# One PSUM tensor of eight banks instead of two fixed groups, with a new task order, in a rope-attention and mixer kernel

## The chip, the core and the metric

The kernel runs on one core of a Trainium2 chip. The metric is device time in microseconds of one execution. Time before: 646.65 us, the median of 3 runs (645.56 to 647.14).

The engines are PE (matrix products), DVE (vector), ACT (scalar and exponential), POOL (general) and SP (issues transfers). They run side by side and wait for each other on semaphores. PE writes its results into PSUM, which has eight banks of 512 floats in each of 128 partitions; DVE and ACT empty a bank, and PE can use it again only then.

## What is computed

```
q, k, v: (4 batches, 8 heads, 576 positions, 64)
q_rot, k_rot = rotate(q), rotate(k)            # x1*cos - x2*sin, x1*sin + x2*cos
scores = (q_rot @ k_rot^T) / sqrt(64)
attn = exp(scores - max);  attn = attn / (sum(attn) + 1e-9)
x = (attn @ v), heads side by side: (4, 576, 512)
h = relu(x^T @ w_tok1) @ w_tok2;  u = x + h^T   # token mixer, width 256
out = u + relu(u @ w_ch1) @ w_ch2               # channel mixer, width 1536
```

The mixer weights come as 64-bit floats and are split on the chip into a high and a low part of 32 bits (`f64_split`); products that need the accuracy take three passes, high by high, high by low and low by high.

## The kernel before, in words

**Two programs, one after the other.** `attention` and the splitting of the token weights (`tok_weights`) are planned together; then `mixers` runs the token and the channel mixer. Each is a list of tasks. `Plan.run` replays the list with estimated durations: on each engine it takes, among the tasks that can start within `SLACK` of the first possible start, the one with the lowest priority number, and emits it. The order of instructions on every engine is fixed by that. The priorities are 9 times the number of the pair plus a number out of the table `AT`.

**Pairs.** The 32 heads are worked on two at a time: 16 pairs, numbered from 0. In this document the tasks of a pair have short names (lines of the kernel before):

- uk and uq: k and q, rotated by POOL (by DVE for pair 0, in two parts: rows 0 to 1 and rows 2 to 4 of a partition; lines 303 to 309), are turned by ten PE transposes (L332); ACT writes the high part (L346), DVE the low part (L349). Until DVE has read it, the bank is held.
- S0, S1, S2, S3: scores of 128 positions of both heads, 12 matmuls each (L431). Each fills two scores tiles, and a scores tile is two banks. DVE's "mx" (L384) copies a scores tile to SBUF, negates it and finds the maximum; that frees the two banks. ACT's "ex" (L388) then makes the exponentials.
- SN: scores of the last 64 positions of both heads, 6 matmuls into one scores tile (L402).
- T0a, T0b to T3a, T3b and TN: transposes of the exponentials, 8, 10 and 10 of them (L451, L413), each task into two single banks. One copy for each bank takes them to SBUF (L456, L418, L422), on ACT or on DVE as the planner thinks it ends first.
- PV0, PV1: attention times v (L469), into one bank; one copy takes it out (L472). In the trace one such matmul is two rows.
- F: the result is turned back by ten transposes (L498) and scaled by DVE (L503, L507).

**Banks.** The scores have two tiles of two banks of their own (`s_ps`), taken in turn; everything else shares four single banks (`t_ps`). So two scores tiles at most are in flight, and four of the others.

**Start.** Tables of cosine and sine come in two transfers from ACT's queue, one pair for k and one (with the factor 1/8 of the scores in it) for q, and four small transfers for the last rows (lines 245 to 248). The q, k and v of a pair come from SP's queue, a large transfer and two small ones each (L278, L282, L285).

## Time and profile before

| | us |
|---|---|
| median of 3 runs | 646.65 |
| the profiled execution, its own time | 648.51 |
| its span, first to last instruction | 646.7 |
| PE busy in the span | 610.4 (94%) |
| DVE busy | 436.4 (67%) |
| ACT busy | 320.6 (50%) |
| POOL busy | 210.5 (33%) |

How to read it: attention fills the first 272 us and the mixers the rest. Busy shares over the whole span mix the two. A PE that counts as busy may be doing matmuls at half rate or issuing them with small gaps between, so the places where PE stands are read from the starts of its instructions in order of time.

### The profile page before, as it was taken

The numbers are of one execution on the slowest core, as the hardware profiler recorded it, in microseconds if no ns is written. First come the engines' busy times: TensorE is split into PE (matmuls) and PEld (weight loads), VectorE is DVE, ScalarE is ACT, GpSimd is POOL, SyncE is SP. The second block draws the span as 40 slices with busy tenths as digits, with TensorE's granted clock in tenths as the row PEclk, the third lists the DMA queues.
The fourth block names the chain that finished last, engine by engine and source line by source line (L and its number), as shares of the span: only waits on it lengthen the run. The fifth ranks groups of instructions, "written<-read, shape, count | busy, mean of one in ns | idle before, by whom it ended". The sixth has DMA issues, their size and how long they took to land.

```text
span 646.7 us, 13245 instructions
## 1 busy us (share of the span) xinstructions
PE 610.4 (94%) x5112; PEld 510.0 (79%) x5112; DVE 436.4 (67%) x1003; ACT 320.6 (50%) x825; POOL 210.5 (33%) x257
## 2 busy tenths in 40 slices
PE   2989999999999999799999999999999999999997
PEld 1766777777777777577879889889989988998995
DVE  4699999988788887499658896379533853233322
ACT  2789889898888888544226542124201410110110
POOL 3968888887766660123021111010000100000000
PEclk9999999999999999989999999999999999999999
DMA  6632322222222020021001422013000100001212
GB/s 181 184 93 61 95 69 60 62 61 80 62 61 61 21 94 3 1 64 59 1 11 64 122 74 58 0 66 96 35 1 1 65 1 0 1 1 65 82 50 98
DMA packets 33439, 36.57 MB, mean 57 GB/s; under 512 B 13792, under 2 KB 26848, under 8 KB 33376
## 3 DMA queue, kind: packets, MB, share of 16 engines
q1 hardware_dynamic: 32512, 35.01, 18.5%
q8 instruction: 40, 0.66, 0.4%
q10 hardware_dynamic: 864, 0.72, 0.3%
q14 instruction: 23, 0.19, 0.1%
HBM read 31.00 MB, written 4.72 MB: 55 GB/s over the span
## 4 chain that ended last, share of the span: by engine, by line
PE 52%; DVE 4%; ACT 1%; issue 0%; POOL 0%; ACTq 0%
PE m L740 22%; PE m L763 22%; PE m L679 3%; PE m L657 3%; DVE xs L640 1%; PE m L718 1%; DVE fh L545 0%; DVE fh L551 0%; DVE rs L665 0%; DVE fa L549 0%; DVE X L682 0%; DVE c1l L558 0%; DVE ul L721 0%; DVE fa L543 0%; DVE fa L547 0%
## 5 line engine op out<-in xcount | busy, mean ns | idle before, releaser
L742 ACT ACTIVATE gh<-m 128x384 fp32r<-128x384 f32 x72 | 35.4, 492 | 188.1 <-PE m L740 158.9
L388 ACT ACTIVATE p<-p,nm 128x576 f32<-128x576 f32 x128 | 100.1, 785 | 9.6 <-DVE p L384 8.9
L384 DVE TENSOR_SCALAR_CACHE_REDUCE p<-s 128x576 f32<-128x576 f32 x128 | 94.5, 751 | 11.6 <-PE s L431 10.9
L740 PE MATMUL m<-uh,c1h 128*128 128x384 f32 x288 | 97.0, 337 | 0.0
L740 PE MATMUL m<-uh,c1l 128*128 128x384 f32 x288 | 96.6, 336 | 0.0
L740 PE MATMUL m<-ul,c1h 128*128 128x384 f32 x288 | 96.6, 335 | 0.0
L744 DVE SCALAR_TENSOR_TENSOR gl<-m,gh 128x384 fp32r<-128x384 f32 x72 | 39.9, 556 | 75.8 <-ACT gh L742 75.3
L469 PE MATMUL t<-pt,vraw 128*64 128x256 f32 (+1 forms) x640 | 85.3, 413 | 0.8 <-ACT pt L422 0.3
L763 PE MATMUL m<-c2h,gh 128*128 128x512 f32 x216 | 84.9, 393 | 0.2 <-DVE ul L721 0.2
L763 PE MATMUL m<-c2h,gl 128*128 128x512 f32 x216 | 85.1, 394 | 0.0
L763 PE MATMUL m<-c2l,gh 128*128 128x512 f32 x216 | 85.0, 393 | 0.0
L765 DVE TENSOR_TENSOR X<-m,X 128x512 f32<-128x512 f32 x64 | 44.1, 691 | 52.1 <-PE m L763 51.4
L469 PEld LDWEIGHTS t<-pt,vraw 128*64 128x64 f32 x640 | 44.4, 138 | 28.6 <-issue 0.7
L456 ACT COPY pt<-t 128x256 f32<-128x256 f32 (+1 forms) x155 | 55.8, 406 | 20.0 <-PE t L451 19.8
L451 PEld LDWEIGHTS t<-ident,p 64*128 64x128 f32 x1152 | 49.7, 141 | 18.9 <-DVE kl L349 4.7
L451 PE MATMUL t<-ident,p 64*128 64x64 f32 x1152 | 59.6, 230 | 2.3 <-ACT pt L456 1.1
L431 PE MATMUL s<-kh,qh 64*128 64x288 f32 x256 | 57.1, 348 | 1.8 <-DVE p L384 1.6
L456 DVE COPY pt<-t 128x256 f32<-128x256 f32 (+1 forms) x101 | 44.3, 451 | 16.2 <-PE t L451 15.4
L740 PEld LDWEIGHTS m<-uh,c1h 128*128 128x128 f32 x288 | 54.1, 188 | 1.1 <-ACT uh L720 0.2
L740 PEld LDWEIGHTS m<-ul,c1h 128*128 128x128 f32 x288 | 54.1, 188 | 0.9
L740 PEld LDWEIGHTS m<-uh,c1l 128*128 128x128 f32 x288 | 54.1, 188 | 0.0
L431 PE MATMUL s<-kl,qh 64*128 64x288 f32 x256 | 49.7, 309 | 0.0
(125 smaller groups left out, 1191.1 us busy)
## 6 DMA issues: line engine op xcount, KB each, us to landing
stg<-in_moe_w_ch_dram SPq DMA_DIRECT2D x16, 384.0 KB, 3.2
stg<-in_moe_w_ch_dram SPq DMA_DIRECT2D x12, 512.0 KB, 4.0
kraw<-in_k_dram SPq DMA_DIRECT2D x16, 256.0 KB, 2.8
qraw<-in_q_dram SPq DMA_DIRECT2D x16, 256.0 KB, 2.8
vraw<-in_v_dram SPq DMA_DIRECT2D x16, 256.0 KB, 3.0
out_dram<-X SPq DMA_DIRECT2D x16, 256.0 KB, 2.3
stg<-in_moe_w_tok_dram SPq DMA_DIRECT2D x4, 512.0 KB, 4.8
kraw<-in_k_dram SPq DMA_DIRECT2D x32, 32.0 KB, 2.5
```

The costliest lines, as they stand in the source:

```text
L384: return lambda: nc.vector.tensor_scalar(out=p().rearrange("p (a b) -> p a b", a=2), in0=sb.t[:, :, 0:W2], scalar1=-1.0, scalar2=None, op0 ...
L388: return lambda: nc.scalar.activation(out=p(), in_=p(), func=ACTF.Exp, bias=nm.t, scale=-1.0, accum_out=l())
L431: nc.tensor.matmul(sbs[h].t[:, c, 0:W2], flat(a.t)[halves[h], TL + j * P:TL + (j + 1) * P], flat(m.t)[halves[h], TL * (1 - h) + c * W2:TL ...
L451: nc.tensor.transpose(xy[z].t[:, i * TL:(i + 1) * TL], pb.t[halves[z], c0:c0 + P], ident[halves[z], halves[z]])
L456: return lambda: e(out=pt[c].t[:, R * h:R * h + m, o + z * TL:o + (z + 1) * TL], in_=xy[z].t[:, 0:m * TL].rearrange("p (r s) -> p r s", r=m))
L469: nc.tensor.matmul(ab.t[halves[h], 0:w], vb.t[:, h, r, :], m, start=(r == 0), stop=(r == R))
L657: nc.tensor.matmul(tb.t, a, m, start=(r == 0 and i == 0), stop=(r == R and i == len(lst) - 1))
L740: nc.tensor.matmul(tb.t[:, 0:N], a, m, start=(i == 0), stop=(i == len(lst) - 1))
L742: x = add("ACT", 0.49, lambda f=f, tb=tb: nc.scalar.activation(out=gb.t[0][:, f], in_=tb.t[:, 0:N], func=ACTF.Relu), [x], [tb, gb], pr + f)
L744: y = add("DVE", 0.56, lambda f=f, tb=tb: nc.vector.scalar_tensor_tensor(out=gb.t[1][:, f], in0=tb.t[:, 0:N], scalar=0.0, in1=gb.t[0][:, f ...
L763: nc.tensor.matmul(tb.t, a, m, start=(i == 0), stop=(i == len(lst) - 1))
L765: y = add("DVE", 0.69, lambda u=u, tb=tb: nc.vector.tensor_tensor(out=u, in0=tb.t, in1=u, op=ALU.add), [z] + sums.get((ci, x), []), [tb], ...
```

## The change

- PSUM is one tensor of eight banks (class `Banks`). A scores tile takes two neighbours beginning at an even bank, every other task takes single banks, and the planner picks the bank that is free first; for single ones at a tie it prefers a bank whose neighbour is taken.
- A scores task reserves its DVE targets (the maxima and the tile for the exponentials) when it is planned, and not when mx is.
- The two copies out of TN's bank are one task, both on the same engine.
- The tables for q are dropped: the factor 1/8 moves into mx's multiplier. What is left comes in two transfers by rows (0 to 1, then 2 to 4) and one small one that waits for both.
- The large transfer of pair 0's k is split into rows 0 to 1 and 2 to 3; its first rotation waits for the first part alone. S0 and S1 of pair 0 wait for the first part of q alone.
- `AT` and `SLACK` have new numbers (PE's slack 0.332 in place of 0.065), which gives another order on every engine. The number of PE instructions stays the same, and in the mixers PE's order has no difference.

```diff
+class Banks:
+    def __init__(self, tile, n):
+        self.tile = tile
+        self.free = {i: 0.0 for i in range(n)}
+        self.made = 0
+    def pick(self, free, two, now):
+        if two:
+            c = min(((max(x, free[i + 1]), i) for i, x in free.items() if i % 2 == 0 and i + 1 in free), default=None)
+            return c and (c[0], (c[1], c[1] + 1))
+        c = min(((max(x, now), i ^ 1 in free, x, i) for i, x in free.items()), default=None)
+        return c and (c[2], (c[3],))
...
-AT = {'load': [-830.1, -824.37, -769.97], 'rot': [-930.58, 206.32], 'pt': [-93.3, -920.53], 'bd': [-226.39], ...
+AT = {'load': [428.08, 436.6, 926.66], 'rot': [418.96, 847.53], 'pt': [599.57, 525.47], 'bd': [314.07], ...
-SLACK = {'PE': 0.065, 'ACT': 0.047, 'DVE': 0.002, 'POOL': 0.135, 'SP': 0.211}
+SLACK = {'PE': 0.332, 'ACT': 0.026, 'DVE': 0.047, 'POOL': 0.235, 'SP': 0.078}
...
-        tabs = pers.tile([P, 4, R + 1, D], F32, name="tabs")
+        tabs = pers.tile([P, 2, R + 1, D], F32, name="tabs")
...
-        s_ps = slots("s", 2, [P, 2, 512], pool=psum)
-        t_ps = slots("t", 4, [P, 512], pool=psum, fifo=False)
-        a_ps = t_ps
-        nc.scalar.dma_start(out=tabs[:, 0:2], in_=tab[0:2].rearrange("a p r d -> p a r d"))
-        nc.scalar.dma_start(out=tabs[:, 2:4], in_=tab[2:4].rearrange("a p r d -> p a r d"))
-        for j in range(4):
-            nc.scalar.dma_start(out=tabs[TL:P, j, R], in_=tab[j, 0:TL, R])
+        banks = Banks(psum.tile([P, 8, 512], F32, name="s"), 8)
+        for r0, r1 in ((0, 2), (2, R + 1)):
+            nc.scalar.dma_start(out=tabs[:, :, r0:r1], in_=tab[0:2, :, r0:r1].rearrange("a p r d -> p a r d"))
+        nc.scalar.dma_start(out=tabs[TL:P, :, R], in_=tab[0:2, 0:TL, R].rearrange("a p d -> p a d"))
...
-                l = [add("SP", 0.5, ld, bufs=[rb], prio=pl)]
+                rows = ((0, 2), (2, R)) if n == 0 and nm == "k" else ((0, R),)
+                l = [add("SP", 0.5, ld(*x), bufs=[rb], prio=pl) for x in rows]
...
-                x = l
+                x = l[0:1] if n == 0 else l
...
-                return lambda: nc.vector.tensor_scalar(out=p().rearrange("p (a b) -> p a b", a=2), in0=sb.t[:, :, 0:W2], scalar1=-1.0,
+                return lambda: nc.vector.tensor_scalar(out=p().rearrange("p (a b) -> p a b", a=2), in0=sb.t[:, :, 0:W2], scalar1=-D ** -0.5,
...
-                t = add("PE", 0.9, qk, qd + kd, [*sbs, qh, ql, kh, kl], g + AT["qk"][i], mode="row")
+                t = add("PE", 0.9, qk, qp[0 if j < 2 else -1] + kd, [*sbs, qh, ql, kh, kl, *nmb, pb], g + AT["qk"][i], mode="row")
```

**PE at the start.** Before, PE turns the second part of pair 0's q (the last rows L332) and then begins S0 (L431); `t` and `s` are the PSUM tiles.

```order
L332 MATMUL t_144<-ident,uq_100 128x64
L332 MATMUL t_145<-ident,uq_100 128x64
L431 MATMUL s_140<-kh_102,qh_106 128x288
L431 MATMUL s_141<-kh_102,qh_106 128x288
L431 MATMUL s_140<-kl_104,qh_106 128x288
L431 MATMUL s_141<-kl_104,qh_106 128x288
L431 MATMUL s_140<-kh_102,ql_108 128x288
L431 MATMUL s_141<-kh_102,ql_108 128x288
```

Now `s` is the one PSUM tensor; L367 are the transposes of k and q, L469 the scores.

```order
L367 MATMUL s<-ident,uk_99 128x64 x10
L367 MATMUL s<-ident,uq_100 128x64 x4
L469 MATMUL s<-kh_102,qh_106 128x288 x2
L469 MATMUL s<-kl_104,qh_106 128x288 x2
L469 MATMUL s<-kh_102,ql_108 128x288 x2
L469 MATMUL s<-kh_102,qh_106 128x288 x2
L469 MATMUL s<-kl_104,qh_106 128x288 x2
L469 MATMUL s<-kh_102,ql_108 128x288 x2
L367 MATMUL s<-ident,uq_100 128x64 x6
```

S0 of pair 0 has moved ahead of the six transposes of q's second part.

**DVE in a middle pair.** Before, the mx (L384) of a pair alternate with copies out of transpose banks (L456) and low parts (L349), at most two of them in a row.

```order
L487 RECIPROCAL ri_129<-l_126 128x10
L456 COPY pt_120<-t_143 128x4x64
L384 TENSOR_SCALAR p_114,nm_135<-s_140 128x576
L456 COPY pt_120<-t_143 128x4x64
L384 TENSOR_SCALAR p_114,nm_138<-s_141 128x576
L384 TENSOR_SCALAR pq_117,nm_137<-s_140 128x576
L456 COPY pt_120<-t_143 128x5x64
L456 COPY pt_120<-t_142 128x5x64
L349 TENSOR_TENSOR ql_109<-t_144,qh_107 128x5x64
L349 TENSOR_TENSOR ql_109<-t_145,qh_107 128x5x64
```

Now L421 is mx and L494 the copy.

```order
L525 RECIPROCAL ri_129<-l_126 128x10
L494 COPY pt_120<-s 128x5x64
L421 TENSOR_SCALAR p_113,nm_136<-s 128x576
L421 TENSOR_SCALAR p_113,nm_132<-s 128x576
L421 TENSOR_SCALAR p_114,nm_137<-s 128x576
L421 TENSOR_SCALAR pq_117,nm_138<-s 128x576
L421 TENSOR_SCALAR p_114,nm_139<-s 128x576
L421 TENSOR_SCALAR p_115,nm_133<-s 128x576
L421 TENSOR_SCALAR p_115,nm_135<-s 128x576
L494 COPY pt_121<-s 128x4x64
```

Seven mx of S0, S1, SN and S2 stand in a row. On PE, S0, S1, SN, S2 and PV1 of the pair before follow each other, and ACT has the seven ex in a row.

**PE between S3 and PV0 of a middle pair.** Before, between S3 of one pair (the first row) and S0 of the next (the last) stand T0b (`p_113`), T1a (`p_114`), F (`oT`) and T1b; rows of a kind that follow are left out.

```order
L431 MATMUL s_141<-kh_103,ql_109 128x288
L451 MATMUL t_142<-ident,p_113 128x64
...
L451 MATMUL t_144<-ident,p_114 128x64
...
L498 MATMUL t_142<-ident,oT_123 128x64
...
L451 MATMUL t_145<-ident,p_114 128x64
L431 MATMUL s_140<-kh_102,qh_106 128x288
```

Now the row L469 ends S3, and L507 is PV0 of the same pair.

```order
L469 MATMUL s<-kh_102,ql_108 128x288 x2
L489 MATMUL s<-ident,p_113 128x64 x10
L489 MATMUL s<-ident,p_114 128x64 x18
L450 MATMUL s<-ident,pq_117 128x64 x10
L489 MATMUL s<-ident,p_115 128x64 x18
L367 MATMUL s<-ident,uq_100 128x64 x10
L536 MATMUL s<-ident,oT_122 128x64 x10
L367 MATMUL s<-ident,uk_99 128x64 x10
L507 MATMUL s<-pt_121,vraw_97 64x256 x10
```

The transposes of the next pairs' k and q, TN, F and all of T0b to T2b stand in one run of 86; before, the longest run is the 38 shown. PE's array mode (`mode` in the tasks: row for transposes and scores, full for SN, column for PV) changes six times in a pair in both kernels.

## Rows read from the trace of the kernel before

**Rows 1.** Busy time by stretch: length, each engine's busy us, PE's granted clock, transfers.

```profile
0.00:14.35 14.35, 1.88 (x20) 1.35 (x22) 6.93 (x23) 2.75 (x8) 3.15 (x25) 1.00 0.63 179
14.35:32.95 18.60, 17.37 (x154) 14.13 (x152) 11.52 (x30) 12.35 (x34) 17.21 (x21) 1.00 0.62 179
32.95:172.25 139.30, 130.84 (x1823) 99.33 (x1819) 128.46 (x338) 124.11 (x348) 110.00 (x126) 1.00 0.26 72
172.25:247.89 75.64, 72.11 (x1038) 55.44 (x1034) 60.97 (x178) 64.87 (x186) 47.40 (x61) 1.00 0.19 56
247.89:272.25 24.36, 22.09 (x289) 16.54 (x285) 14.64 (x46) 16.83 (x50) 0.49 (x2) 1.00 0.01 2
272.25:646.70 374.45, 366.12 (x1816) 323.20 (x1816) 213.87 (x396) 99.73 (x201) 32.28 (x24) 0.99 0.14 44
```

**Rows 2.** PE's waits: line, for whom, us in total, times, longest.

```profile
PE s L402 <- DVE p L384: 4.8, 11, 1.2
```

**Rows 3.** PE in order of time, one pair: start, us, instruction [idle before, releaser].

```profile
192.26 0.71 PE L451 MATMUL t<-ident,p 64*128 64x64 f32 x18
193.37 0.50 PE L402 MATMUL s<-kh,bd 128*128 128x288 f32 x2 [0.40 <-DVE p L384]
...
194.33 0.52 PE L332 MATMUL t<-ident,uq 64*128 64x64 f32 x10
...
194.97 0.68 PE L431 MATMUL s<-kh,qh 64*128 64x288 f32 x2
...
196.03 0.63 PE L332 MATMUL t<-ident,uk 64*128 64x64 f32 x10
196.59 2.91 PE L469 MATMUL t<-pt,vraw 128*64 128x320 f32 x20
199.44 0.46 PE L451 MATMUL t<-ident,p 64*128 64x64 f32 x8
199.71 0.38 PE L431 MATMUL s<-kh,qh 64*128 64x288 f32 x2
...
200.59 0.72 PE L451 MATMUL t<-ident,p 64*128 64x64 f32 x18
201.57 0.79 PE L498 MATMUL t<-ident,oT 64*128 64x64 f32 x9 [0.26 <-ACT pt L456]
202.20 0.22 PE L451 MATMUL t<-ident,p 64*128 64x64 f32 x1
```

**Rows 4.** DVE in order of time, the same pair.

```profile
192.46 0.76 DVE L384 TENSOR_SCALAR_CACHE_REDUCE p<-s 128x576 f32<-128x576 f32 x1 [0.39 <-PE s L431]
...
196.80 0.75 DVE L384 TENSOR_SCALAR_CACHE_REDUCE p<-s 128x576 f32<-128x576 f32 x1
...
197.47 0.75 DVE L384 TENSOR_SCALAR_CACHE_REDUCE p<-s 128x576 f32<-128x576 f32 x1
...
200.78 0.76 DVE L384 TENSOR_SCALAR_CACHE_REDUCE p<-s 128x576 f32<-128x576 f32 x1 [0.39 <-PE s L431]
```

**Rows 5.** ACT's copies in order of time, the same pair.

```profile
192.76 1.03 ACT L456 COPY pt<-t 128x320 f32<-128x320 f32 x3 [0.56 <-PE t L451]
```

**Rows 6.** The start in order of time: DVE and PE.

```profile
4.84 0.43 DVE L303 TENSOR_TENSOR w<-kraw,tabs 128x256 f32<-128x256 f32 x1 [4.84 <-DMA tabs<-in_tab_dram]
7.65 0.56 DVE L303 TENSOR_TENSOR w<-kraw,tabs 128x384 f32<-128x384 f32 x1 [1.53 <-DMA tabs<-in_tab_dram]
14.35 0.58 PE L431 MATMUL s<-kh,qh 64*128 64x288 f32 x2
16.17 0.76 DVE L384 TENSOR_SCALAR_CACHE_REDUCE p<-s 128x576 f32<-128x576 f32 x1 [0.49 <-PE s L431]
```

**Rows 7.** PE in order of time at the end of attention.

```profile
270.83 0.40 PE L498 MATMUL t<-ident,oT 64*128 64x64 f32 x6 [0.24 <-ACT oT L472]
273.28 0.79 PE L657 MATMUL m<-xs,w1h 128*128 128x512 f32 x1 [2.05 <-ACT xs L638]
```

**Rows 8.** Busy time by stretch, as Rows 1: the start of the mixers.

```profile
273.30:280.20 6.90, 6.33 (x14) 4.67 (x15) 6.21 (x11) 3.23 (x7) 2.97 (x2) 0.51 0.00 0
```

More of the change, by code (lines that the diff above doesn't have):

```diff
@@ L30, in __init__ @@
         self.taken = 0
+class Banks:
[9 more added lines that the diff above has]
+        return c and (c[2], (c[3],))
 class Buf:
-    def __init__(self, slots):
+    def __init__(self, slots, two=False):
         self.slots = slots
+        self.two = two
         self.order = slots.made
@@ L87, in start @@
                 sl = b.slots
+                if isinstance(sl, Banks):
+                    free = want.setdefault(sl, dict(sl.free))
+                    c = sl.pick(free, b.two, self.clock["PE"])
+                    if not c:
+                        return None
+                    s = max(s, c[0])
+                    for i in c[1]:
+                        del free[i]
+                    continue
                 k = want[sl] = want.get(sl, -1) + 1
@@ L130, in run @@
             for b in t.bufs:
+                if b.held is None and isinstance(b.slots, Banks):
+                    sl = b.slots
+                    c = sl.pick(sl.free, b.two, self.clock["PE"])
+                    for i in c[1]:
+                        del sl.free[i]
+                    i = c[1][0]
+                    b.held = (c[0], c[1], sl.tile[:, i:i + 2] if b.two else sl.tile[:, i])
                 if b.held is None:
@@ L144, in run @@
                 b.end = max(b.end, end + LAG[eng])
-                if not b.users:
+                if not b.users and isinstance(b.slots, Banks):
+                    b.slots.free.update((i, b.end) for i in b.held[1])
+                elif not b.users:
                     b.slots.free.append((b.end,) + b.held[1:])
@@ L275, in prep, with ld @@
                 tail = a[:, M:S, :].rearrange("h p d -> p h d")
[L277 to L279 removed]
+                def ld(r0, r1, rb=rb, a=a):
+                    return lambda: nc.sync.dma_start(out=rb.t[:, :, r0:r1, :].rearrange("p h r d -> p h (r d)"),
+                                                     in_=a[:, 0:M, :].rearrange("h (p r) d -> p h (r d)", r=R)[:, :, r0 * D:r1 * D])
                 def ldt(o, rb=rb, tail=tail):
@@ L302, in go @@
                         if i == 0:
-                            e.tensor_tensor(out=w, in0=src, in1=bc(c + 1), op=ALU.mult)
+                            e.tensor_tensor(out=w, in0=src, in1=bc(1), op=ALU.mult)
                         elif i == 1:
-                            e.tensor_tensor(out=u, in0=src, in1=bc(c), op=ALU.mult)
+                            e.tensor_tensor(out=u, in0=src, in1=bc(0), op=ALU.mult)
                         elif i == 2:
@@ L312, in prep @@
                 hi, lo = Buf(hls[nm + "h"]), Buf(hls[nm + "l"])
-                x = l
+                x = l[0:1] if n == 0 else l
                 eh, el = [], []
+                part = []
                 for r0, r1 in ((0, 2), (2, R + 1)) if n == 0 else ((0, R + 1),):
+                    if r0:
+                        x = x + l[1:]
                     for i in range(4):
@@ L322, in prep @@
                             x = [add("POOL", pool(w), rot(nc.gpsimd, i), x, bufs, pos + AT["rot"][int(2 * pr)])]
-                    xy = [Buf(t_ps), Buf(t_ps)]
+                    xy = [Buf(banks), Buf(banks)]
                     split = r0 > 0
@@ L353, in prep @@
                             el.append(add("DVE", dve(m * TL), fl, [y], [xy[z], hi, lo], pp))
-                ready[n, nm] = (eh + el, hi, lo)
+                    part.append(eh + el)
+                ready[n, nm] = (part, hi, lo)
                 if nm == "q":
@@ L394, in pair @@
                 if j is None:
-                    xy = [Buf(t_ps), Buf(t_ps)]
-                    sb, nm, pb = Buf(s_ps), Buf(nms), Buf(pqs)
+                    xy = [Buf(banks), Buf(banks)]
+                    sb, nm, pb = Buf(banks, True), Buf(nms), Buf(pqs)
                     def qk(sb=sb):
@@ L422, in cpt @@
                             return lambda: e(out=pt[c].t[halves[z], R, 2 * P:2 * P + TL], in_=xy[z].t[halves[z], R * TL:(R + 1) * TL])
-                        ev[c] += [both(cp, R * TL, [x], [xy[z], pt[c]], at("cp")), both(cpt, 2 * TL, [x], [xy[z], pt[c]], at("cp"))]
+                        two = lambda e, cp=cp, cpt=cpt: lambda: (cp(e)(), cpt(e)())
+                        ev[c].append(both(two, R * TL + 2 * TL + 60, [x], [xy[z], pt[c]], at("cp")))
                     continue
-                sbs, nmb, pb = [Buf(s_ps), Buf(s_ps)], [Buf(nms), Buf(nms)], Buf(ps)
+                sbs, nmb, pb = [Buf(banks, True), Buf(banks, True)], [Buf(nms), Buf(nms)], Buf(ps)
                 def qk(sbs=sbs, j=j):
@@ L443, in pair @@
                 for h in range(2):
-                    xy = [Buf(t_ps), Buf(t_ps)]
+                    xy = [Buf(banks), Buf(banks)]
                     m = R + h
@@ L462, in pair @@
                 c0 = 2 * P * c
-                ab = Buf(a_ps)
+                ab = Buf(banks)
                 def pv(c=c, w=w, ab=ab):
@@ L491, in pair @@
             inv = add("DVE", 0.13, f3, [x], [lb, rb], pi)
-            xy = [Buf(t_ps), Buf(t_ps)]
+            xy = [Buf(banks), Buf(banks)]
             cs = hp * 2 * D
```

15 lines of the change are left out of this document (6 added, 9 removed).

## The prediction

> **What bounds the kernel now.** I read the busy times by stretch first. Attention ends at 272.25 us; the mixers take the other 374.45 us of the span of 646.70, with PE busy for 366.12 of them [rows 1]. PE's order in the mixers has no difference, so I leave that stretch as it is. In attention I cut the stretches where S0 of pairs 0, 1, 10 and 15 begins: 14.35 us of loading and rotating, 18.60 us for the first pair, 139.30 us for nine pairs (15.48 each) and 75.64 us for five pairs (15.13 each) [rows 1]. In the last five PE is busy for 72.11 us, ACT for 64.87, DVE for 60.97: 14.42, 12.97 and 12.19 of 15.13 a pair. PE is nearest to its limit, and no engine is far from it.
>
> A busy PE hides its waits, so I then read PE in order of time through one pair, from start to start [rows 3]. First the prices without a wait: eight transposes 0.27 us (199.44 to 199.71); a scores task 0.88 (199.71 to 200.59); twenty transposes 0.64 (194.33 to 194.97), so ten 0.32; PV1 2.85 (196.59 to 199.44); SN 0.96 (193.37 to 194.33). Against these, four places are late. Eighteen transposes take 1.11 ahead of SN (0.59 without wait, so 0.52 lost; a scores tile comes free only after an mx) and 0.98 ahead of F (0.39 lost, a copy on ACT). F itself takes 0.63 (0.31 lost). S2 takes 1.06 (0.18 lost, half a tile late). Together 1.40 us of 15.13: the work with its changes of array mode needs about 13.73. The list of waits names the same first place, 4.8 us in all for SN behind mx [rows 2].
>
> **The change, part by part.**
>
> *What costs nothing.* Instructions on PE are the same. In a middle pair ACT and DVE have the same instructions too, by kind and number (on ACT nine ex, six copies of 256, five of 320 and four casts). The factor 1/8 rides in mx's multiplier. The joined copies of TN are the same two instructions.
>
> *The start.* DVE's first rotation waits for the tables until 4.84, its second group until 7.65 [rows 6]. The first wait is now for 1024 bytes of tables in each partition where it was 2560, and for half of k; the second for one small transfer, which itself is sent only after two others have landed, where it was for the second of four. I give the second wait 0.7 us less: below 0 if the three landings follow as slowly as now, above 1.5. Then S0 of pair 0 moves ahead of the last six transposes of q. On DVE the low parts of q's first part, which S0 needs last, stand behind two rotations of its second part, as before, but the other two rotations and the three low parts of the second part no longer stand ahead of S0's end. Together I put the first mx of pair 0, 16.17 before [rows 6], 2.1 us earlier (bounds 1.0 and 3.0).
>
> *The first pair.* Now S2 and S3 of pair 0 come early and T3 late, and k and q of pair 1 are turned together after T2. Following bank by bank I find pair 1's S2 another 2.8 us earlier, if nothing slips; this stretch also holds the splitting of the first token weights, which fills gaps on ACT and DVE that this count needs. I take 1.5 (bounds 0 and 4).
>
> *A middle pair.* The gain is the four waits above; what has to be found is what is late next. I follow PE through the new order with S0's start as zero, with these lags: mx begins 1.07 us after its scores task (199.71 to 200.78), mx follow each other in 0.67 (196.80 to 197.47), and PE can write the banks 0.91 after an mx began (192.46 to 193.37) [rows 3, 4].
> - S0 and S1 now take all eight banks, one after the other, without a wait. SN needs a bank pair of S0's first mx: 1.07 + 0.91 = 1.98. PE is free at 1.76. Wait 0.22.
> - S2 needs the banks of the third mx: 1.07 + 2 x 0.67 + 0.91 = 3.32. PE is free at 1.98 + 0.96 = 2.94. Wait 0.38. Behind it on PE stand PV1 and T0a of the next pair, but DVE has three mx in hand meanwhile, and ACT's seven ex (five of them behind the third) end before PV1 does.
> - PV1, T0a, S3 and T0b find their banks empty. T1a too; T1b needs the bank that ACT empties of T0b. ACT's copies begin 0.50 after the transposes (192.26 to 192.76) and three take 1.03 us [rows 3, 5], so one is done some 0.4 later: 0.9 after T0b began, while T0b and T1a take 0.32 + 0.27. Wait 0.35.
> - T2a waits for S3's second mx, and the transposes of k for a copy on DVE, 0.1 each.
> - T3 needs two ex that ACT makes while PE runs PV0 (256 columns where PV1 has 320 in its 2.85 us, so some 2.3): covered, with a few tenths to spare. If ACT is later than this, the next pair's S0 is late by as much.
>
> Together 1.15 us, where it was 1.40. The 0.52 ahead of SN held a change of array mode, and the 0.22 there holds one too, so nothing is left out by this; the smaller hand-overs between scores and PV I put 0.1 lower than now; that is my choice, no row has this pair of tasks. So a pair takes 13.73 + 1.15 - 0.1 = 14.78 us in place of 15.13, 0.35 less. Both ends: 0, if one wait of 0.35 appears that I don't see, and 1.1, if the banks' freedom removes four fifths of the waits (with eight banks shared, the waits that I priced are all on the latency from PE to a copy and back, which a slightly later start of PE shortens). Fourteen pairs from S0 of pair 1 to S0 of pair 15 give 14 x 0.35 = 4.9 us. The token weights' splitting lies in nine of these pairs in both kernels, and makes them 0.35 longer than the others now (15.48 against 15.13); I leave that as it is (plus or minus 2 us).
>
> *The end.* From S0 of pair 15 to the mixers 24.36 us [rows 1]. The last pair now has PV1 of pair 14 earlier, and F and PV0 cover the last ex; T3 then needs a copy before the last PV1, as now. I leave it at 0.
>
> *The sum.* 2.1 + 1.5 + 4.9 = 8.5 us less. The profiled execution has a span of 646.7 and a time of 648.51, 1.8 around it and 0.3% above the median of 646.65; a new profile should show a span near 638.2. From the median: 646.65 - 8.5 = **638.1 us**.
>
> **The rivals.**
>
> *The waits only move.* DVE's seven mx in a row and ACT's late copies could cost as much as the four waits did, since each wait that I found is a latency and not a free choice. Speaking for it: in both kernels PE has to hand a scores tile to DVE and take it back nine times a pair. Then only the start is gained, 2.1 + 1.5: 643.0 us.
>
> *The banks free PE almost wholly.* The pair goes to 14.0 to 14.2 us, near the 13.73 of work, and the first pair follows my count in full: 2.1 + 2.8 + 14 x 0.9 = 17.5 less, 629.2. For it: ACT and DVE need only 12.97 and 12.19 a pair. Against it: the two waits behind mx of S0 and S1 can be computed and don't go away.
>
> *PE's clock falls in the run of transposes.* In the record before, the clock fell once. Six transposes at 270.83, then PE stood for 2.05 us until 273.28 [rows 7], and from about then until 280.2 the granted clock was 0.51, the lower of 1.2 and 2.4 GHz [rows 8]. So some 2.5 microseconds or more with nothing but transposes and idle time came ahead of the fall. Before, the longest such stretch inside a pair is the 38 transposes from T0b at 200.59 to the end of T1b, which begins at 202.20 [rows 3] and takes 0.3: 1.9 us. Now it is a run of 86, at 0.032 each 2.8 us, with 0.55 of waits 3.3 us in each pair. A fall of 6.9 us at half speed loses 3.4 us of PE's work. Three of them undo the gain; one in every second pair gives 638.1 + 7 x 3.4 = 662 us. Against it: in this run PE stands still for only some tenths at a time, where before the fall it stood for 2.05 us. The Trainium skill's page "TensorE: Matmul & The Clock Gate", section "A second HAM failure mode: psum-queue depth-cycling", describes a kernel that cycles through PSUM banks in each iteration, with small idle gaps of PE between groups, and whose clock went up and down for it. By that rule this kernel would lose; the trace before agrees only so far as that banks were waited for in every pair and the clock stayed up in all of them.
>
> **How the numbers follow.** The forecast (630 to 642 with its own bounds) has 0.50, the waits that only move 0.20, PE almost free 0.15, the falling clock 0.12; 0.03 is left for an order that is slower for another reason. The range goes from 630 to 645.5: it takes in the bounds of the first three and leaves out the falling clock and the lowest times of the third, together under 0.2. A measurement of this kernel tells a difference of some 0.3% (2 us) from none. Faster by more than that: nearly all of the first three, 0.81. Within it: 0.06, from the upper end of the moved waits. Slower: 0.13, the falling clock and the rest.
>
> **What the new profile would show.** The start: the first mx near 14.1 us. The pairs: S0 to S0 in the last five stretches near 14.8 us, with waits of SN and S2 behind mx of 0.2 and 0.4, and of T1b behind a copy on ACT; no wait of F. The clock: granted 1.00 through attention. The mixers: 374 us from their first cast. I would be wrong if PE waits in T3 for ex (ACT would be the bound), if S0 of a middle pair waits for a low part of k on DVE, or if the granted clock falls inside a pair.

## The result, and the profile after

The changed kernel takes 638.39 us (median of 4, 636.89 to 639.87), against 646.89 for the kernel before in the same session: a ratio of **0.9861, 95% interval 0.9833 to 0.9889**. 638.1 was predicted. Run again later (experiment n) it gave 0.9882 (0.9861 to 0.9903).

The stretches of the changed kernel's profile, bounded as in [rows 1] by S0 of pairs 0, 1, 10 and 15, the end of attention and the end; columns as there:

```profile
0.00:12.76 12.76, 1.53 (x15) 1.00 (x16) 5.98 (x20) 2.75 (x8) 2.83 (x24) 1.00 0.58 157
12.76:29.18 16.42, 14.37 (x183) 11.93 (x184) 14.19 (x42) 13.48 (x38) 12.64 (x16) 1.00 0.61 179
29.18:167.26 138.08, 130.94 (x1860) 99.20 (x1858) 128.95 (x338) 123.20 (x354) 115.11 (x131) 1.00 0.27 75
167.26:241.09 73.83, 72.34 (x1038) 54.81 (x1034) 60.63 (x176) 63.40 (x186) 50.40 (x63) 1.00 0.22 61
241.09:261.00 19.91, 17.68 (x223) 13.05 (x218) 12.76 (x39) 12.60 (x37) 0.49 (x2) 1.00 0.01 2
261.00:634.80 373.80, 365.15 (x1816) 322.20 (x1816) 213.63 (x395) 99.69 (x201) 32.02 (x24) 1.00 0.14 44
```

Five late pairs take 73.83 us, 14.77 each, where [rows 1] had 15.13. The nine pairs ahead of them shrink by only 1.22 us. The last stretch shrinks by 4.45, but look at the counts of PE's instructions: 183, 1860 and 223 in the first pair, the nine pairs and the last stretch, where [rows 1] has 154, 1823 and 289. In the new order more of a pair is done when the next S0 begins, so these three stretches do not hold the same work as before. Only their sum can be compared: 182.26 us before, 174.41 now.

PE in order of time through one late pair, as in [rows 3]:

```profile
196.81 0.38 PE L469 MATMUL s<-kh,qh 64*128 64x288 f32 x2
...
197.68 0.72 PE L469 MATMUL s<-kh,qh 64*128 64x288 f32 x2
...
198.65 0.41 PE L469 MATMUL s<-kh,ql 64*128 64x288 f32 x2
198.99 0.54 PE L439 MATMUL s<-kh,bd 128*128 128x288 f32 x2
...
199.98 0.48 PE L469 MATMUL s<-kh,qh 64*128 64x288 f32 x2
...
200.75 0.37 PE L469 MATMUL s<-kh,ql 64*128 64x288 f32 x2
201.05 2.91 PE L507 MATMUL s<-pt,vraw 128*64 128x320 f32 x20
...
204.16 0.38 PE L469 MATMUL s<-kh,qh 64*128 64x288 f32 x2
204.38 0.29 PE L469 MATMUL s<-kl,qh 64*128 64x288 f32 x2
204.51 0.29 PE L469 MATMUL s<-kh,ql 64*128 64x288 f32 x2
...
204.91 0.29 PE L469 MATMUL s<-kh,ql 64*128 64x288 f32 x2
205.04 0.72 PE L489 MATMUL s<-ident,p 64*128 64x64 f32 x18
206.03 0.56 PE L489 MATMUL s<-ident,p 64*128 64x64 f32 x10 [0.27 <-ACT pt L494]
...
207.29 0.54 PE L367 MATMUL s<-ident,uq 64*128 64x64 f32 x10
207.63 0.67 PE L536 MATMUL s<-ident,oT 64*128 64x64 f32 x10
208.08 0.67 PE L367 MATMUL s<-ident,uk 64*128 64x64 f32 x10
208.68 2.38 PE L507 MATMUL s<-pt,vraw 128*64 128x256 f32 x20
```

From start to start, less the prices of the prediction: S1 takes 1.31 until SN (0.43 lost; 0.22 was counted), T0b and T1a take 0.99 until T1b (0.40; 0.35), F takes 0.45 (0.13; none). The starts inside the scores tasks tell more. In S3 the last two matmuls start 0.75 us after the first two (204.16 to 204.91). In S1 it is 0.97 (197.68 to 198.65), so 0.22 of the 0.43 is a delay inside S1 that was not counted, and 0.21 stands ahead of SN, with the change of array mode. In S2 it is 0.77 (199.98 to 200.75): the wait of 0.38 that was forecast for S2 is not there.

S2 takes 1.07 until PV1 and uk 0.60 until PV0, 0.19 and 0.28 above their prices. This is the hand-over to PV, and the kernel before has two of these as well: uk takes 0.56 until PV1 [rows 3], 0.24 above its price, and TN takes 0.52 until PV0, 0.20 above the 0.32 of ten transposes. The 13.73 us of the prediction hold them already, so they are no new loss. TN and PV0 before:

```profile
203.39 0.59 PE L413 MATMUL t<-ident,pq 64*128 64x64 f32 x10
203.91 1.30 PE L469 MATMUL t<-pt,vraw 128*64 128x256 f32 x10
```

The start, as in [rows 6], DVE and PE:

```profile
3.63 0.43 DVE L335 TENSOR_TENSOR w<-kraw,tabs 128x256 f32<-128x256 f32 x1 [3.63 <-DMA tabs<-in_tab_dram]
7.64 0.56 DVE L335 TENSOR_TENSOR w<-kraw,tabs 128x384 f32<-128x384 f32 x1 [2.73 <-DMA tabs<-in_tab_dram]
...
13.16 0.44 PE L469 MATMUL s<-kl,qh 64*128 64x288 f32 x2
13.40 0.44 PE L469 MATMUL s<-kh,ql 64*128 64x288 f32 x2
...
14.61 0.76 DVE L421 TENSOR_SCALAR_CACHE_REDUCE p<-s 128x576 f32<-128x576 f32 x1 [0.90 <-PE s L469]
```

The first wait for tables ends 1.21 us earlier, the second where it did (7.65 before). The first mx comes 1.56 us earlier.

Here two scores matmuls take 0.24 us (13.16 to 13.40), where in the late pair they take 0.13 (204.38 to 204.51): PE starts at the lower of its two clocks. The trace's record of the granted clock rises at 16.79 us in this profile; in that of the kernel before it rose at 30.98 us. The record begins with that rise, so the clock's column shows 1.00 for the time ahead of it too, here and in [rows 1], although the clock was the lower one there.

What holds up the nine pairs shows best in one of them, pair 6. ACT, DVE, POOL and PE in order of time:

```profile
115.19 1.11 ACT L595 CAST w2h<-fh 128x512 fp32r<-128x512 f32 x1 [1.63 <-DVE fh L589]
...
110.95 1.25 DVE L587 TENSOR_TENSOR fa<-fc,fa 128x512 f32<-128x512 f32 x1
112.12 1.09 DVE L579 TENSOR_SCALAR fa<-fa 128x512 f32<-128x512 f32 x1
113.13 2.03 DVE L589 TENSOR_TENSOR fh<-fh,fa 128x512 f32<-128x512 f32 x1
115.09 0.95 DVE L581 TENSOR_SCALAR fa<-fa 128x512 uint32<-128x512 uint32 x1
115.95 0.74 DVE L421 TENSOR_SCALAR_CACHE_REDUCE p<-s 128x576 f32<-128x576 f32 x1
...
113.00 1.61 POOL L335 TENSOR_TENSOR w<-kraw,tabs 128x640 f32<-128x640 f32 x1
...
116.69 0.60 PE L489 MATMUL s<-ident,p 64*128 64x64 f32 x10 [2.52 <-ACT pt L494]
```

Four operations of the splitting of a token weight stand in a row on DVE, from 110.95 to 115.95. The planner reckons with 0.68, 0.42, 0.68 and 0.42 us for them (`0.0012 * n + 0.07` and `0.0007 * n + 0.06` with n = 512), 2.20 in all; they take 5.00. (The planner also starts such a task only when POOL is free by its own reckoning, `port` in the kernel; on the chip POOL was at work beside all four.) ACT's cast waits for the third, the copies behind the cast wait with it, and PE stands for 2.52 us in its run of transposes.

### The profile page after: what moved, and what is told of

Its sections match the earlier page's. It is cut to its first block, busy times and chain, and to the rows that moved or that the text cites. A ratio compares the mean times of both kernels' runs of the same rounds, so it can differ in the third digit from the quotient of the medians.

```text
span 634.8 us, 13288 instructions
## 1 busy us (share of the span) xinstructions
PE 602.0 (95%) x5112; PEld 502.2 (79%) x5112; DVE 436.1 (69%) x1004; ACT 315.1 (50%) x821; POOL 213.5 (34%) x260
## 4 chain that ended last, share of the span: by engine, by line
PE 51%; DVE 5%; ACT 1%; issue 0%
PE m L778 23%; PE m L801 23%; PE m L717 3%; PE m L695 2%; DVE xs L678 1%; PE m L756 1%; DVE fh L583 0%; DVE fh L589 0%; DVE rs L703 0%; DVE fa L587 0%; DVE X L720 0%; DVE c1l L596 0%; DVE ul L759 0%; DVE fa L581 0%; DVE fa L585 0%
## 5 line engine op out<-in xcount | busy, mean ns | idle before, releaser
L425 ACT ACTIVATE p<-p,nm 128x576 f32<-128x576 f32 x128 | 98.0, 770 | 13.2 <-DVE p L421 13.2
L421 DVE TENSOR_SCALAR_CACHE_REDUCE p<-s 128x576 f32<-128x576 f32 x128 | 90.6, 752 | 7.0 <-PE s L469 6.6
L507 PE MATMUL s<-pt,vraw 128*64 128x256 f32 (+1 forms) x640 | 85.4, 411 | 0.3 <-DVE pt L494 0.3
L507 PEld LDWEIGHTS s<-pt,vraw 128*64 128x64 f32 x640 | 44.7, 137 | 28.4 <-DVE pq L421 1.3
L489 PEld LDWEIGHTS s<-ident,p 64*128 64x128 f32 x1152 | 45.8, 138 | 26.1 <-ACT pt L494 8.2
L489 PE MATMUL s<-ident,p 64*128 64x64 f32 x1152 | 54.9, 229 | 8.9 <-ACT pt L494 6.2
L494 ACT COPY pt<-s 128x256 f32<-128x256 f32 (+1 forms) x167 | 56.9, 412 | 10.8 <-PE s L489 10.6
L469 PE MATMUL s<-kh,qh 64*128 64x288 f32 x256 | 52.8, 337 | 1.9 <-ACT pt L494 0.6
L494 DVE COPY pt<-s 128x320 f32<-128x320 f32 (+1 forms) x89 | 38.5, 450 | 16.4 <-PE s L489 15.7
L801 PEld LDWEIGHTS m<-c2h,gl 128*128 128x128 f32 x216 | 40.6, 188 | 9.2
```

The costliest lines, as they stand in the source:

```text
L421: return lambda: nc.vector.tensor_scalar(out=p().rearrange("p (a b) -> p a b", a=2), in0=sb.t[:, :, 0:W2], scalar1=-D ** -0.5, scalar2=Non ...
L425: return lambda: nc.scalar.activation(out=p(), in_=p(), func=ACTF.Exp, bias=nm.t, scale=-1.0, accum_out=l())
L469: nc.tensor.matmul(sbs[h].t[:, c, 0:W2], flat(a.t)[halves[h], TL + j * P:TL + (j + 1) * P], flat(m.t)[halves[h], TL * (1 - h) + c * W2:TL ...
L489: nc.tensor.transpose(xy[z].t[:, i * TL:(i + 1) * TL], pb.t[halves[z], c0:c0 + P], ident[halves[z], halves[z]])
L494: return lambda: e(out=pt[c].t[:, R * h:R * h + m, o + z * TL:o + (z + 1) * TL], in_=xy[z].t[:, 0:m * TL].rearrange("p (r s) -> p r s", r=m))
L507: nc.tensor.matmul(ab.t[halves[h], 0:w], vb.t[:, h, r, :], m, start=(r == 0), stop=(r == R))
```

## The experiments

**New start alone, old start, old banks, old numbers (a to d).** Four parts taken alone or away, the planner left to plan.

a, on the kernel before: all hunks of the diff that touch the tables, k's load, mx's factor and S0's dependency.

```diff
-        tabs = pers.tile([P, 4, R + 1, D], F32, name="tabs")
+        tabs = pers.tile([P, 2, R + 1, D], F32, name="tabs")
...
-                t = add("PE", 0.9, qk, qd + kd, [*sbs, qh, ql, kh, kl], g + AT["qk"][i], mode="row")
+                t = add("PE", 0.9, qk, qp[0 if j < 2 else -1] + kd, [*sbs, qh, ql, kh, kl], g + AT["qk"][i], mode="row")
...
```

> The kernel before with the new start alone: two tables in two transfers by rows, the factor 1/8 in mx, pair 0's k loaded in two parts, S0 and S1 of pair 0 on the first part of q; banks, AT and SLACK as before. Theory (the start gains what it gained in the changed kernel, whose first mx came at 14.61 us where before it came at 16.17): first mx between 14.2 and 15.2 us, S0 of a late pair still every 15.1 us, ratio 0.9965 to 0.998 of before. Rival (a gain at the start is eaten in the first pairs, where k and q of pairs 1 and 2 come from POOL at their own pace): first mx earlier all the same, but S0 of pair 2 where it was, ratio 0.999 to 1.001.

Measured: ratio 1.0507 (1.0485 to 1.0528), a miss for both theories. S0 of pair 0 did come early, at 12.82 us (before 14.35), but the late pairs take 16.7 to 16.9 us, and the granted clock falls in none of these (it fell three times ahead of them, for 3.41 us each). The start had put the planner's replay into another order in every pair, with these numbers a bad one; h below holds the order and shows that the start itself is not slow.

b, on the changed kernel: the same hunks taken back.

```diff
-                rows = ((0, 2), (2, R)) if n == 0 and nm == "k" else ((0, R),)
+                rows = ((0, R),)
...
-                t = add("PE", 0.9, qk, qp[0 if j < 2 else -1] + kd, [*sbs, qh, ql, kh, kl, *nmb, pb], g + AT["qk"][i], mode="row")
+                t = add("PE", 0.9, qk, qp[-1] + kd, [*sbs, qh, ql, kh, kl, *nmb, pb], g + AT["qk"][i], mode="row")
...
```

> The changed kernel with the start of before: four tables and their six transfers, one transfer for pair 0's k, the factor 1/8 in the tables, S0 of pair 0 behind all of q. Theory (the start is worth its 1.6 us and nothing hangs on it): first mx near 16 us, S0 to S0 in the last pairs 14.8 us, ratio 0.988 to 0.990 of before where the changed kernel has 0.986. Rival 1 (start is eaten later): 0.986. Rival 2 (the early start carries the first pair too, 3 us or more): 0.991 or above. The granted clock: by the theory it rises early in this order too, near 17 to 20 us, since S0, S1 and SN of pair 0 stand one behind another here, where in the kernel before the transposes and ex of S0 came between and it rose at 30.98 us.

Measured: 0.9917 (0.9896 to 0.9938). S0 of pair 0 at 14.52 us, the late pairs 14.76: with this start the new numbers give late pairs of the same length. The nine pairs ahead of them have another order, though (pairs 4 and 5 take 17.98 and 17.01 us where the changed kernel has 15.26 and 14.76), so b is no measurement of the start alone. By its ratio it is 2.3 us behind the repeated changed kernel (n), and its interval doesn't part the theory from rival 2. The clock rose at 18.77 us, as expected, but fell at 25.59 and at 87.03, for 3.41 us each. The reason that was given for the early rise isn't shown by it: with one and the same order the changed kernel rose early in one profile and late in another (n, below).

c and d, on the changed kernel: the two groups of banks, and the old `AT` and `SLACK`.

```diff
-        banks = Banks(psum.tile([P, 8, 512], F32, name="s"), 8)
+        s_ps = slots("s", 2, [P, 2, 512], pool=psum)
+        t_ps = slots("t", 4, [P, 512], pool=psum, fifo=False)
...
```

```diff
...
-SLACK = {'PE': 0.332, 'ACT': 0.026, 'DVE': 0.047, 'POOL': 0.235, 'SP': 0.078}
+SLACK = {'PE': 0.065, 'ACT': 0.047, 'DVE': 0.002, 'POOL': 0.135, 'SP': 0.211}
```

> The changed kernel with the two groups of banks of before (two scores tiles of two banks, four single banks), with its new AT and SLACK. Theory (banks and numbers gain only together: with two scores tiles S1 cannot follow S0, so the planner has to put PV1 or transposes between them): S0 to S0 in the last pairs 15.0 to 15.6 us in place of 14.77, ratio 0.994 to 1.004 of before. Rival (the numbers are the gain, the banks are not needed): 14.8 us and 0.986 to 0.989.

> The changed kernel with the AT and SLACK of before: eight banks in one pool, old numbers. Theory (banks and numbers gain only together): S0 to S0 in the last pairs 15.0 to 15.4 us, ratio 0.993 to 1.002 of before, of which some 0.0025 is the start. Rival (the shared banks are the gain, whatever the order): 14.8 us or less and 0.985 to 0.989.

Measured: c 1.0652 (1.0619 to 1.0684), d 1.0452 (1.0426 to 1.0479); late pairs of 15.2 to 22.8 and of 16.0 to 16.3 us. Both rivals are false, and the theory's size is too. As a, these two say nothing of banks or numbers by themselves: each makes the planner find another order. The granted clock also fell inside attention, in d five times, for 27.3 us together, in c three times, for 13.7.

**The order held fast (f to i).** So the order was taken out of the planner's hands. The tasks are replayed from a list for each engine; a task still gets its buffers when it is planned, and the hardware waits as it must.

```diff
+SCRIPT = {"PE":[8,17,31,519,40,530, ...
...
+Plan.run = lambda self: replay(self) if SCRIPT else planned(self)
```

f is the kernel before with its own order and `Banks`, g the changed kernel with its own order and the two groups of banks (the diff of c), h the kernel before with its own order and the new start (the diff of a), i the changed kernel with its own order and without the splits (constants stand in for the token weights, so i does not compute the result):

```diff
     def tok_weights(places):
...
+        for t in (w1h, w1l, w1th, w1tl, w2h, w2l):
+            w1_done.append(add("POOL", 1.0, lambda t=t: nc.gpsimd.memset(t.bitcast(F32), 0.01), [x_done[2][-1]]))
...
```

> The kernel before with the order of its instructions on every engine held fast (the list of tasks is replayed), and only the banks changed: one pool of eight, scores tiles two neighbours, as in the class Banks. Theory (the order is what uses the freedom; with the old order the tasks seldom find a bank earlier): S0 to S0 in the last pairs 14.9 to 15.15 us where it was 15.12, ratio 0.994 to 1.000. Rival (the shared banks are the gain by themselves): 14.1 to 14.7 us, ratio 0.975 to 0.989.

> The changed kernel with its order held fast, PE's, DVE's, POOL's and SP's row by row (in pair 0 a few copies of ACT change places, since its order needs six single banks there), and only the banks changed back: two scores tiles of two banks, four single ones. Theory (this order lives on the eight banks): S1 must wait for both mx of S0, SN for an mx of S1, S2 for SN's; by the lags of the prediction S2 ends 7.4 us after S0 began in place of 4.2 to 4.4, and the run of transposes waits for copies on top: S0 to S0 in the last pairs 17.5 to 20.5 us, ratio 1.06 to 1.13. Rival (the order is the gain, the banks are not needed): 14.8 to 15.0 us, ratio 0.986 to 0.992.

Measured: f **1.0000** (0.9983 to 1.0017), the rival false. PE's waits in the five late pairs of f, and in those of the kernel before, each with us in total, times and longest:

```profile
PE s L435 <- DVE p L417: 1.9, 5, 0.4
PE s L531 <- ACT pt L489: 1.3, 5, 0.3
```

```profile
PE s L402 <- DVE p L384: 1.9, 5, 0.4
PE t L498 <- ACT pt L456: 1.3, 5, 0.3
```

SN waits as long for a free pair among eight banks as it did among four, and F for a copy. With the old order these two tasks find no bank earlier. The granted clock fell once inside attention in f, at 43.33 for 3.41 us.

g: **1.2019** (1.1972 to 1.2066), the theory's sign and more than its size; late pairs of 21.7 to 25.8 us, 23.9 on the mean. The busy times of one such pair, and PE in it in order of time:

```profile
299.04:322.96 23.92, 19.39 (x214) 13.62 (x210) 12.71 (x36) 13.76 (x38) 10.64 (x13) 0.86 0.15 40
```

```profile
300.99 0.40 PE L470 MATMUL s<-kh,qh 64*128 64x288 f32 x1 [0.86 <-DVE p L422]
301.67 0.39 PE L470 MATMUL s<-kh,qh 64*128 64x288 f32 x1 [0.28 <-DVE p L422]
...
303.67 0.82 PE L440 MATMUL s<-kh,bd 128*128 128x288 f32 x2 [0.95 <-DVE p L422]
...
306.31 1.28 PE L470 MATMUL s<-kh,qh 64*128 64x288 f32 x2 [0.86 <-DVE pq L422]
...
308.72 3.61 PE L508 MATMUL t<-pt,vraw 128*64 128x320 f32 x20
```

S1, SN and S2 each wait for an mx, as expected. What the theory left out stands in the clock's column: 0.86. The granted clock fell at 303.34, for 6.83 us, while PE waited for SN's tile, and PV1 ran part of its 3.61 us (2.91 in the changed kernel) at the lower rate. Inside attention it fell 15 times, for 102 us together; at half speed that loses up to 51 (an estimate) of the 138 us by which attention is longer than in the changed kernel. No run took out the reservation of DVE's targets or the joined copies of TN by themselves.

> The kernel before with its order held fast on PE, DVE and POOL, and the start changed: two tables in two transfers by rows and one small one, 1/8 in mx, pair 0's k in two parts. S0 of pair 0 still stands behind all of q's transposes. Theory (the 5% that the new start cost with the old numbers came from another order of the whole plan, and the loads are worth about a microsecond): first mx 14.8 to 15.7 us, S0 to S0 in the last pairs 15.1 us, ratio 0.997 to 0.9995. Rival (something in the new start itself is slow, a multiplier in mx or the loads): ratio above 1.01.

> The changed kernel with its order held fast, without the splitting of the token weights: their transfers and the tasks of f64_split in attention are left out, the six tiles of weights get a constant from POOL, and so the mixers work on other weights. Theory (the splitting is what makes nine middle pairs 15.34 us where the last five take 14.77: its operations stand in the way on DVE and ACT): the nine pairs from S0 of pair 1 to S0 of pair 10 take 132.9 to 133.8 us in place of 138.08, ratio 0.977 to 0.981 of before. Rival (the early pairs are slow for another reason, transfers or the order): 136.5 us or more, ratio 0.983 to 0.987.

Measured: h 0.9984 (0.9969 to 1.0000). The loads and the factor are worth about a microsecond, nothing in them is slow, and a's 5% came with the other order. i 0.9795 (0.9772 to 0.9818), as the theory has it. The nine pairs of i:

```profile
30.84:164.10 133.26, 129.97 (x1861) 98.99 (x1858) 106.83 (x311) 115.44 (x339) 98.14 (x119) 1.00 0.24 67
```

133.26 us where they took 138.08 with the splits: the splitting costs 4.8 us, and nothing else makes these pairs longer than the late ones by more than 0.04 each.

**Two ways to have more, and the changed kernel again (j to n).** j moves the splits by hand, k loads the tables' last rows so that no transfer overlaps another, l does both, n changes nothing. The order is held in j to l.

```diff
-        for r0, r1 in ((0, 2), (2, R + 1)):
+        for r0, r1 in ((0, 2), (2, R)):
             nc.scalar.dma_start(out=tabs[:, :, r0:r1], in_=tab[0:2, :, r0:r1].rearrange("a p r d -> p a r d"))
-        nc.scalar.dma_start(out=tabs[TL:P, :, R], in_=tab[0:2, 0:TL, R].rearrange("a p d -> p a d"))
+        for o in range(2):
+            nc.scalar.dma_start(out=tabs[o * TL:(o + 1) * TL, :, R], in_=tab[0:2, 0:TL, R].rearrange("a p d -> p a d"))
```

> The changed kernel with its order held fast, PE's row by row, and only the 68 tasks that split the token weights placed by hand: over pairs 1 to 15 in place of 0 to 8, in each pair at most some 1.6 us of them on DVE (in the gap of 1.53 us behind the mx of S2), one or two on ACT (before the first ex of S0, and before the copies of T0b), and the multiplications, additions and last subtractions on POOL (in its gap of 3.14 us). Theory (the splits cost 4.8 us because several of them stand together and are longer than planned; spread over the gaps they cost little): the nine pairs from S0 of pair 1 to S0 of pair 10 take 133.3 to 135.5 us in place of 138.08, pairs 10 to 14 at most 14.95 each, ratio 0.978 to 0.983 of before. Rival (their work on DVE and ACT costs PE wherever it is put, since neither has time to spare near the scores): nine pairs 136.5 us or more, or the last five longer by as much, ratio 0.985 or above.

> The changed kernel with its order held fast and the tables' last rows loaded so that no transfer waits for another: rows 0 to 1, rows 2 to 3, and the last rows twice, for the lower and the upper partitions; in the changed kernel the small one was sent at 4.71 us, behind the landing of the two large ones at 3.61 and 4.63, and landed at 7.62. Theory (that one wait holds DVE's second group of rotations until 7.64): the second group begins at 5.2 to 6.2 us, the first mx of pair 0 at 12.4 to 13.4 (14.61 in the changed kernel), and the execution is 1.2 to 2.2 us shorter than the changed kernel's: ratio 0.982 to 0.985. Rival (k's own small transfers or q's loads end the wait at nearly the same time, or the first pair takes back what the start gives): second group 7 us or later, or S0 of pair 1 less than 0.6 us earlier, ratio 0.9855 to 0.988.

> Both: the splits in the gaps and the tables' last rows apart. Theory (they add): 2.5 to 6.5 us below the changed kernel, ratio 0.976 to 0.982 of before. Rival (one of the two gives nothing): ratio 0.983 to 0.986.

> The changed kernel once more, beside the other three. Theory: ratio 0.984 to 0.988 again, S0 to S0 in the last pairs 14.77 us; the moment at which the granted clock rises in the first pair is not the same from run to run (16.79 us in the first profile; 24.6 us in the run without splits, whose PE order is the same), so it may lie anywhere from 16 to 26 us here, and the first pair is up to 2 us longer when it is late. Rival (the early rise belongs to this order): 16.5 to 17.5 us again.

Measured: j 0.9895 (0.9872 to 0.9917), k 0.9845 (0.9821 to 0.9870), l 0.9856 (0.9832 to 0.9880), n 0.9882 (0.9861 to 0.9903).

j by stretches (nine pairs, five pairs, the end):

```profile
30.77:165.40 134.63, 130.31 (x1864) 99.06 (x1858) 117.02 (x325) 122.50 (x351) 110.42 (x128) 1.00 0.28 75
165.40:240.37 74.97, 72.55 (x1036) 54.87 (x1034) 68.96 (x186) 66.63 (x191) 58.48 (x68) 1.00 0.21 60
240.37:265.00 24.63, 21.70 (x223) 14.23 (x218) 12.26 (x36) 13.32 (x38) 3.33 (x6) 0.86 0.00 1
```

The nine pairs came out as the theory said, 3.45 us shorter. The five late ones came out 1.14 longer; one of these took 15.73 us, above the 14.95 that was expected at most. The end took all of it back: 24.63 us where the changed kernel has 19.91. In the last pair PE has three waits of 0.52 to 0.61 us in its run of transposes that the changed kernel hasn't, the clock fell at 253.14 for 6.83 us, and ACT's last cast of a split waited 2.90 us for POOL, whose last splits I had put behind the row that waits for pair 15's last exponentials. So j neither beats the changed kernel nor shows the rival: the nine pairs gained, and my placement at the end lost as much. How the loss divides between the waits and the clock was not taken apart.

l has nearly the same stretches: nine pairs of 134.42 us, five of 74.95, and 25.1 us from S0 of pair 15 to the first matmul of the mixers, where k has 20.6. The two do not add in it, and the theory is false. The ratio is the rival's, but not its reason: the start and the nine pairs gave what they should, and j's part lost it again in the late pairs and at the end.

k: the second group of rotations begins at 5.95 us, S0 of pair 0 at 11.07.

```profile
5.95 0.56 DVE L336 TENSOR_TENSOR w<-kraw,tabs 128x384 f32<-128x384 f32 x1 [0.97 <-DMA tabs<-in_tab_dram]
...
11.07 0.61 PE L470 MATMUL s<-kh,qh 64*128 64x288 f32 x2 [0.52 <-ACT qh L382]
```

S0 of pair 15 is still 1.83 us ahead of where the first profile of the changed kernel has it (the clock rose 3.6 us after the first S0 here, 4.0 there). So the theory holds in the trace. k is the fastest of these, 637.79 against 639.45 us for n in the same session, as long a step as expected; but the intervals of the two ratios overlap, so the times alone don't show it.

n: S0 of pair 0 at 12.66, the late pairs 14.77, and the rival false: the clock rose at 24.01 us, and it fell inside attention. PE in pair 6, and the clock's column from 119.60 on:

```profile
119.14 0.62 PE L489 MATMUL s<-ident,p 64*128 64x64 f32 x10 [2.51 <-ACT pt L494]
```

```profile
119.60:123.00 3.40, 3.40 (x65) 3.28 (x61) 2.83 (x9) 2.87 (x10) 0.06 (x1) 0.50 0.02 5
```

It is the stall of pair 6 again, in the run of transposes, and here the clock fell 0.44 us after it, at 119.58, for 3.41 us. The same happened at 71.79, for 3.41 us, in pair 3. In the first profile both stalls were there and the clock stayed up.

## Why the prediction was right, point by point

Each stretch, from the profiles before [rows 1], after, and of n (which ends its attention at 264.40 and its span at 638.3):

| | before | after | n | change | predicted |
|---|---|---|---|---|---|
| to S0 of pair 0 | 14.35 | 12.76 | 12.66 | -1.6, -1.7 | -2.1 |
| first pair, nine pairs and end | 182.26 | 174.41 | 177.92 | -7.85, -4.34 | -4.65 |
| five late pairs | 75.64 | 73.83 | 73.82 | -1.8, -1.8 | -1.75 |
| mixers | 374.45 | 373.80 | 373.90 | -0.65, -0.55 | 0 |
| span | 646.70 | 634.80 | 638.3 | -11.9, -8.4 | -8.5 |

*The middle pair* (15.13 to 14.78) was measured at 14.77. The mechanism is the predicted one: the long waits for banks are gone, and short ones on the way from PE to a copy and back are left. On the prediction's own terms they add up to some 1.05 us, as it had them, but they are divided otherwise. SN (0.21 for 0.22) and T1b (0.40 for 0.35) are as forecast. S2 waits 0.02 and not 0.38, and the hand-overs to PV are not 0.1 shorter (0.17 and 0.28, where before they are 0.24 and 0.20); S1's 0.22 and F's 0.13, for which nothing was counted, fill the place. So the sum is right to 0.01 by luck, since these errors cancel. f and g show what the prediction did not ask: banks alone give nothing, and the order without the banks costs 20%. The gain belongs to neither alone.

*The start* was sized too large: 2.1 us were forecast for the first mx, which came 1.56 earlier. The term that failed is the 0.7 us of the second wait: the small transfer for the last rows overlaps the second large one, so it was sent only at 4.71, after both had landed. The prediction had named that wait and given it a lower bound below 0; k shows that it was worth 1.7 us.

*The first pair, and the end.* These two terms, -1.5 and 0, cannot be told apart, because the stretches between marks S0 hold other work now (183 and 223 PE instructions for 154 and 289). That was a fault of the marks: at S0 they are comparable only if the order around them is. In sum with the nine pairs, -4.65 was predicted, and the two profiles give -7.85 and -4.34. The kernel before was profiled with its clock rising late, at 30.98 us; the prediction, with the 1.00 of [rows 1] for that time, put this at nothing. f, with the same order and the same start, rose at 22.85 and needed 15.16 us for the first pair in place of 18.60; h rose at 20.46 and needed 15.50. So some 3 us of the first figure is the clock and not the change. With 15.16 or 15.50 for the first pair before, the change to the first profile is -4.4 to -4.75 (an estimate), near what was forecast. In n the clock works against the change as well: it rose late (first pair 17.79 for 16.42) and fell twice.

*The splits of the token weights* were left as they are, plus or minus 2 us. They cost some 3.1 us before (139.30 less nine times 15.13; no run of the old order is without them) and 4.8 now (i). So the nine pairs gave 1.22 us by their marks where 3.15 was forecast. And each stall that the splits make in the transposes can bring the clock down with it: the nine pairs of n took 140.26 us, longer than before.

*The mixers* were put at 0 and came out 0.65 and 0.55 us shorter. It need not be the change: about where they begin the clock fell for 6.83 us before, and for 3.41 in the first profile and in n. f, which has the mixers of before, fell there for 3.41 us; from their first matmul to the end it took 372.58 us, the kernel before 373.40, the changed kernel 373.08 and n 373.12.

*The sum.* 646.89 less 638.39 is 8.5 us, as forecast. That it fits so well is luck in part: the start gave 0.5 less, the mixers some 0.6 that nobody counted, and the two profiles of the changed kernel lie 3.5 us apart.

*The falling clock* (chance 0.12). The run of 86 transposes does not bring the clock down by itself, as that rival had it: the first profile, k and i show no fall inside their sixteen pairs, n none in the other fourteen. In n it fell in two pairs in which PE stood in that run, for 0.43 and 0.93 us in pair 3 and for 2.51 in pair 6; in the first profile PE stood as long in both, and the clock stayed up. The new order isn't needed for it either: f, with the order of before, has its fall after 28 transposes with waits of 0.20 and 0.76 us and one scores task. The price was for a fall of 6.9 us, 3.4; those of n lasted 3.41, and the pairs took 17.21 and 18.43 us where the first profile has 16.03 and 17.35: 1.2 and 1.1 us each, less than half of their length. The Trainium skill's page "TensorE: Matmul & The Clock Gate", section "A second HAM failure mode: psum-queue depth-cycling", has the clock go up and down in a kernel that cycles through PSUM banks with small idle gaps of PE. The late pairs here don't agree with it (banks cycle in each, with losses of 0.1 to 0.4 us at a place); g, where SN waits some 0.9 us for its banks in fifteen pairs, does, with its 15 falls.

Against the signs that were named: the first mx came at 14.61 and not 14.1; S0 to S0, the waits of SN and T1b, and the mixers are there; the wait of S2 is not, and F lost 0.13 us. The granted clock did not fall inside attention in the first profile, and fell twice in n.

## What to carry to other kernels

A freer allocation and the order that uses it are one change. To learn which of them pays, hold the order fast and change the other: an experiment that lets a greedy planner plan anew tests another order each time. Three of the four here came out 4 to 7% slower, and for one of these (a) the run with the order held (h) shows that the part itself was not slow.

Marks that divide a pipelined loop into stretches must stand at the same place in the work; compare the instruction counts of the stretches before comparing their times. And one profile of each kernel is not enough where the clock moves: here the same order with the same start differed by 3.4 us in the first pair (18.60 before, 15.16 in f).

## What the runs showed of the hardware

**When the clock rises.** PE's order is one and the same in these six profiles. The granted clock rose from the lower to the higher level at very different moments, and the first pair is 1.0 to 1.6 us longer where it rose late (times in us):

| | S0 of pair 0 | clock rises | first pair |
|---|---|---|---|
| k | 11.07 | 14.69 | 16.23 |
| changed kernel | 12.76 | 16.79 | 16.42 |
| l | 11.01 | 19.95 | 17.39 |
| n | 12.66 | 24.01 | 17.79 |
| j | 12.99 | 24.45 | 17.78 |
| i | 13.06 | 24.60 | 17.78 |

No row shows why it rose when it did.

**DVE beside POOL.** The same addition of 512 columns, L589, ran twice on DVE: in 2.03 us at 113.13 (above), and here in 0.68, with POOL's rows around it:

```profile
137.37 0.68 DVE L589 TENSOR_TENSOR fh<-fh,fa 128x512 f32<-128x512 f32 x1
...
136.49 0.23 POOL L398 CAST bd<-qh 64x64 fp32r<-64x64 f32 x1
137.96 0.26 POOL L522 TENSOR_SCALAR l<-l 128x10 f32<-128x10 f32 x1 [1.24 <-ACT l L519]
```

At 137.37 POOL stood still, until 137.96. At 113.13 it had just begun a rotation (113.00), which ended at 114.61, 1.48 us after DVE's start; 1.48 and 0.68 make 2.16, near the 2.03. So it looks as if DVE's operation waited for POOL's to end. The Trainium skill's page "SBUF — State Buffer", section "SBUF: two separate sides", has the two engines share a pair of ports that whichever begins first holds for its whole instruction, on DVE's side among others for operations with two inputs in SBUF, as this addition has; these two rows agree with it. The shift of 512 columns, L581, goes the same way: 0.41 us at 28.02, with nothing on POOL, and 0.95 at 115.09, beside a subtraction on POOL that ended at 115.75. No experiment here moved POOL's work away from this place alone.
